# A second-attention-layer K tile group as seven block products, and a new order for all queues, on one Trainium2 core

## The chip, the core and the metric

The kernel runs on one core of one Trainium2 chip. The core has five instruction queues that run side by side: TensorE (PE, with its weight loads shown as PEld), VectorE (DVE), ScalarE (ACT), GpSimd (POOL) and SyncE (SP, which here only issues transfers). Each queue executes its instructions strictly in the order in which they were written; between queues there are only semaphores. The metric is the device time of the whole program in microseconds (us): the median of several runs. Beside it stands one profiled run, from which all durations come.

## The reference

The input is one sequence x of 2048 rows and 512 columns in bf16, with two sets of weights. Four layers follow each other: linear attention, feed-forward, and the same two once more with the same weights.

```python
x = x + attn(layernorm(x), wqkv, wo)     # layer 0
x = x + ffn(layernorm(x), w1, w2)        # layer 1
x = x + attn(layernorm(x), wqkv, wo)     # layer 2
x = x + ffn(layernorm(x), w1, w2)        # layer 3

def attn(x, wqkv, wo):                   # 32 heads of 16 columns
    q, k, v = split(x @ wqkv)
    phi = lambda t: where(t > 0, t + 1, exp(t)) + 1e-6
    kv  = sum over rows of phi(k)^T v    # 16 x 16 for each head
    z   = sum over rows of phi(k)
    return ((phi(q) @ kv) / (phi(q) @ z + 1e-6)) @ wo

def ffn(x, w1, w2):                      # 512 -> 1376 -> 512
    return maximum(x @ w1, 0) @ w2
```

## The kernel before, in words

The 2048 rows are held as 16 tiles of 128 rows, in four chunks of four tiles. Everything stays on the chip between the layers. In an attention layer each chunk is normalised, transposed (`Tb`), and multiplied with the K and Q columns of `wqkv`; `phi` of the K product is kept by tiles (`big`, used as PE's stationary operand later) and `phi` of the Q product by chunks. The products of `phi(k)` with the rows (`g0_*`, `g1_*`), the column sums (`zcol`, which becomes `Zc`), the head products (`kv*`, masked into `KVT` on DVE at L1133) and the merged matrix `Mf` (`m0` to `m3`, evicted at L1140 and L1141) form a barrier: the output of the layer (`fin*`, `ps<-Mf,big`) can only start when all rows have gone into them. For the denominator of chunk t, `den<t>` multiplies `phi(q)` by `Zc` (`ps<-big,Zc`), ACT takes a logarithm (`lnd<t>`, L1189) and an exponential of its negative (`rdc<t>`, L1191), SP spreads the result over the heads by four transfers of 128 KB (`spread<t>_*`, L1201, `big<-rdc`), and DVE multiplies two column blocks at a time (`pqs<t>_0` and `pqs<t>_2`, L1209). The `fin` products of chunk t need its two `pqs`.

The start is a special case. PE first multiplies a matrix of zeros by itself (`warm`, L793, `ps<-wrm`, WARM times 512 columns), and later eight times 128 columns (`fill0`, L816). The first tiles' statistics are DVE's `bnst<i>` and `bnag<i>` (L821, L822), ACT's `lnv<i>` and `rstd<i>` (L827, L829) and DVE's `fnorm<i>` (L859). The transposes of these tiles are made by PE (`trp<i>`, L888) and copied out of PSUM by ACT or DVE (L894, L895); those of later chunks by transfers (L874).

A block product replaces eight products of quarter matrices by seven, at the price of sums. In the feed-forward layers it is used for both matmuls, and in layer 2 for Q and K of chunks 0, 1 and 2. The list `A7` says which. A plain K chunk is four groups of four matmuls of 512 columns (`kproj12` to `kproj15`), each evicted by ACT once as t + 1 (L907) and once as exp(t) (L909) and joined on DVE (L915, L917). A block K chunk is seven groups (`k7_<chunk>_1` to `_7`) of four matmuls of 256 columns. Before them stand four sums of quarters of `Tb` on DVE (`as1` to `as4`, L996), which chunk by chunk serve Q and K alike; between them ACT copies one partial result into a second bank (`seed`, L681) and saves two (L1022), and DVE adds these back (L1042); ACT and DVE then do the same t + 1, exp, clamp and maximum (L1040, L1055, L1057, L1065, L1066).

The order is not that of the program's text. Every operation is entered into a graph with a name, and a list scheduler places the operations on each engine by priority:

```python
op.prio = op.idx + HINTS.get(op.key, 0)
...
pend = {e: sorted((o for o in ops if e in engs_of(o)), key=lambda o: (o.prio, o.idx)) for e in ENGINES}
```

`HINTS` has one number for each of some 1,850 operations (key: layer and name). An entry whose key ends in `!` picks the engine where an operation could go to several. The scheduler runs a model of the times to see what is ready and which PSUM bank comes free; its constants (`LOAD_LATE`, how late a load lands; the cost handed over with each matmul group) enter the order in that way and do nothing on the chip themselves. The result is one fixed order for each queue.

Of the kernel before, what the change touches and what calls it, by code (L numbers as in the profile page):

```python
# [52 lines left out]
LOAD_LATE = {"x1": -350.0, "x2": 190.0, "wka": 380.0, "wkb": 490.0, "wqa": 450.0, "x4": 500.0, "wqb": 510.0, "x12": 410.0, "x8": 260.0, "wv0": 350.0}  # L53
# [8 lines left out]
HINTS = {"0.as1": 50, "0.as3": 144, "0.as_h1": 145, "0.as_h2": 183, "0.as_id": 2, "0.bnag0": -4, "0.bnag1": -14, "0.bnag10":  # L62
# [525 lines left out]


def build_kernel(nc, A_x, A_wqkv, A_wo, B_w1, B_w2, out, n_layers_pairs=2, K_STT=0, Q_STT=0, windows=None,  # L590
                 WARM=10, SPLIT0=True, FIRST_PE_CHUNKS=2,
                 flex_strict=True, flex_bias_dve=0.0):
    FLEX_STRICT[0] = flex_strict
    FLEX_BIAS[DVE] = flex_bias_dve
# [16 lines left out]
    with es:  # L611
# [27 lines left out]
        Zc = sb("Zc", [128, 4, 32], BF16)  # L639
# [1292 lines left out]
```

## Time and profile before

| | us |
|---|---|
| median of 3 runs | 265.5 (265.16 to 266.06) |
| the profiled run's own time | 265.44 |
| its span, first to last instruction | 263.4 |
| outside the span | 2.04 |
| PE busy | 257.8 (98% of the span) |
| DVE busy | 225.7 (86%) |
| ACT busy | 198.8 (75%) |
| POOL busy | 59.4 (23%) |

The span is what the profile explains; the 2.04 us outside it are in every run. PE's busy time lies so near the span that the question at each place is whether PE waits there, and if it does, for which of the other queues. The chain of waits in the profile follows the last instruction back through what released it; where that chain is on PE for a long stretch, PE ran without a break. A row `178.09 12.22 PE L927 MATMUL ps<-Mf,big ... x55` of the timeline reads: starts at 178.09 us, lasts 12.22 us to the end of the last, matmuls of line 927 into PSUM from the stationary `Mf` and the moving `big`, 55 of them. Since matmuls overlap in the array, the spacing of n in a row is the length, less that of a single one, over n - 1.

### The profile page before, as it was taken

How to read it: one execution, taken by the hardware profiler on the slowest of the kernel's cores; microseconds unless marked ns; L12 is line 12 of the kernel's file. 1: busy time of each engine (PE TensorE's matmuls, PEld its weight loads, DVE VectorE, ACT ScalarE, POOL GpSimd, SP SyncE). 2: the span in 40 equal slices, each digit the busy share in tenths (PEclk: the TensorE clock that was granted, in tenths of full speed). 3: DMA queues.
4: the chain of work that ended last, by engine and by line, in shares of the span. 5: the costliest groups of instructions: out<-in, count | busy, mean ns of one | idle time of the engine just before them, and what ended most of it. 6: DMA issues, size and time to landing. Idle time of an engine off the chain costs nothing.

```text
span 263.4 us, 5741 instructions
## 1 busy us (share of the span) xinstructions
PE 257.8 (98%) x2130; PEld 194.2 (74%) x2130; DVE 225.7 (86%) x562; ACT 198.8 (75%) x429; POOL 59.4 (23%) x166
## 2 busy tenths in 40 slices
PE   7999999999999999999999999999999999999994
PEld 2744446844788898988888875574479988889883
DVE  4997795799999989998989988369998998888884
ACT  3999999469999888798998799776999943265000
POOL 1211000027942014122160430003891400000000
PEclk9999999999999999999999999999999999999999
DMA  6653982724415018232406031076437102400204
GB/s 218 260 147 76 256 317 64 178 54 93 91 43 102 1 20 122 40 24 43 39 0 82 0 64 20 2 163 157 80 60 141 24 2 81 80 2 35 67 0 162
DMA packets 45980, 22.46 MB, mean 85 GB/s; under 512 B 35872, under 2 KB 44416, under 8 KB 45952
## 3 DMA queue, kind: packets, MB, share of 16 engines
q1 hardware_dynamic: 45680, 21.83, 35.8%
q8 instruction: 17, 0.28, 0.4%
q10 hardware_dynamic: 272, 0.26, 0.4%
q14 instruction: 11, 0.09, 0.1%
HBM read 7.14 MB, written 2.10 MB: 35 GB/s over the span
## 4 chain that ended last, share of the span: by engine, by line
PE 93%; ACT 2%; DMA 2%; DVE 1%; issue 0%; SPq 0%; DVEq 0%
PE ps L927 92%; DMA big<-rdc 1%; DMA xin<-in_A_x_dram 1%; ACT rdc L1191 1%; PE ps L888 1%; ACT lnd L1189 1%; DVE bst L821 0%; DVE big L1209 0%; DVE big L1066 0%; ACT escr L909 0%; ACT GT L1121 0%; ACT big L907 0%; PE ps L816 0%; DVE rdc L1582 0%; DVE xn L859 0%
## 5 line engine op out<-in xcount | busy, mean ns | idle before, releaser
L942 ACT ACTIVATE sqscr<-xres 128x512 bf16<-128x512 f32 x48 | 29.9, 624 | 4.6 <-DVE xres L934 4.0
L681 ACT ACTIVATE ps<-ps 128x512 f32<-128x512 f32 (+1 forms) x38 | 20.6, 543 | 16.6 <-PE ps L927 13.4
L927 PE MATMUL ps<-w,big 128*128 128x256 bf16 (+1 forms) x256 | 32.7, 272 | 0.0
L927 PE MATMUL ps<-big,xn 128*128 128x256 bf16 (+1 forms) x224 | 32.1, 288 | 0.0
L927 PE MATMUL ps<-Mf,big 128*128 128x512 bf16 x128 | 28.5, 379 | 0.0
L927 PEld LDWEIGHTS ps<-w,big 128*128 128x128 bf16 (+1 forms) x256 | 25.0, 98 | 3.0
L927 PEld LDWEIGHTS ps<-big,xn 128*128 128x128 f16 x224 | 21.1, 98 | 7.5 <-issue 1.4
L927 PE MATMUL ps<-Tb,w 128*128 128x256 f16 x160 | 24.5, 273 | 0.0
L927 PE MATMUL ps<-Tb,wqkv 128*128 128x512 f16 (+1 forms) x120 | 23.5, 329 | 0.0
L927 PEld LDWEIGHTS ps<-Mf,big 128*128 128x128 bf16 x128 | 12.2, 98 | 15.3 <-ACT Mf L1140 0.9
L907 ACT ACTIVATE big<-ps 128x512 bf16<-128x512 f32 x40 | 23.0, 640 | 0.6 <-PE ps L927 0.6
L927 PE MATMUL ps<-xn,w 128*128 128x256 f16 x160 | 23.3, 272 | 0.0
L1398 ACT ACTIVATE big<-ps 128x512 bf16<-128x512 f32 (+1 forms) x32 | 17.0, 539 | 8.4 <-PE ps L927 8.2
L927 PE MATMUL ps<-xn,xin 128*128 128x256 f16 x160 | 23.2, 272 | 0.0
L927 PE MATMUL ps<-wqkv,Tb 128*128 128x512 bf16 (+1 forms) x104 | 23.0, 355 | 0.0
L851 POOL TENSOR_TENSOR rstd<-veps,nhalf 128x2 f32<-128x2 f32 x24 | 20.0, 835 | 11.4 <-DVE veps L849 10.4
L1410 DVE TENSOR_TENSOR big<-ps,escr 128x512 bf16<-128x512 f32 (+1 forms) x34 | 20.0, 590 | 2.6 <-PE ps L927 2.1
L1429 ACT ACTIVATE escr<-ps 128x512 f32<-128x512 f32 (+1 forms) x34 | 16.9, 522 | 2.4 <-PE ps L927 2.4
L927 PEld LDWEIGHTS ps<-Tb,wqkv 128*128 128x128 bf16 x120 | 11.6, 98 | 8.7 <-ACT Tb L894 0.4
L843 POOL TENSOR_SCALAR mean<-s 128x2 f32<-128x2 f32 x24 | 6.3, 263 | 49.9 <-DVE xres L934 48.7
L927 PEld LDWEIGHTS ps<-Tb,w 128*128 128x128 bf16 x160 | 15.2, 98 | 2.8 <-DVE w L1358 0.5
L927 PE MATMUL ps<-w,Tb 128*128 128x96 bf16 (+2 forms) x176 | 17.2, 224 | 0.0
(145 smaller groups left out, 599.2 us busy)
## 6 DMA issues: line engine op xcount, KB each, us to landing
big<-rdc SPq DMA_DIRECT2D x32, 128.0 KB, 2.7
xin<-in_A_x_dram SPq DMA_DIRECT2D x3, 512.0 KB, 6.8
w<-in_B_w_dram SPq DMA_DIRECT2D x1, 1376.0 KB, 7.1
w<-in_B_w_dram SPq DMA_DIRECT2D x1, 1280.0 KB, 10.2
wqkv<-in_A_wqkv_dram SPq DMA_DIRECT2D x3, 256.0 KB, 4.3
wqkv<-in_A_wqkv_dram SPq DMA_DIRECT2D x1, 512.0 KB, 4.2
wo<-in_A_wo_dram SPq DMA_DIRECT2D x1, 512.0 KB, 4.3
out_dram<-GT SPq DMA_DIRECT2D x1, 512.0 KB, 2.7
```

The costliest lines, as they stand in the source:

```text
L681: g.add(ACT, lambda e: e.activation(psv[:, b, 0:w], psv[:, src, 0:w], ACTF.Identity), [("ps", src)], [("ps", b)], C_ACT_PSUM if w == 512 e ...
L843: g.add(POOL, lambda e: e.tensor_scalar(mean[:, sl], s1[:, sl], -INV_D, None, ALU.mult), [("s1", i) for i in tl], [("mean", i) for i in tl ...
L851: g.add(POOL, lambda e: e.tensor_tensor(rstd[:, sl], veps[:, sl], nhalf[:, 0:n], ALU.pow), [("veps", lo), ("nhalf",)], [("rstd", i) for i ...
L888: last = e.transpose(psb()[:, 128 * c:128 * c + 128], xn[:, i, 128 * c:128 * c + 128], ident[:])
L907: ops = [g.add(ACT, lambda e: e.activation(dst_ap, psv[:, b, :], ACTF.Identity, bias=1.0 + 1e-6, scale=1.0), [("ps", b)], [dst_key], C_ACT ...
L927: last = e.matmul(o, l, r, start=st, stop=sp, skip_group_check=skip)
L942: g.add(ACT, lambda e: e.activation(sqscr[:, q, :], xres[:, i, :], ACTF.Square, scale=math.sqrt(INV_D), accum_out=s2[:, i:i + 1]), xr(i), ...
L1189: g.add(ACT, lambda e: e.activation(lnd[:, s, :], psv[:, b, :], ACTF.Ln, bias=1e-6, scale=1.0), [("ps", b)], [("lnd", s)], C_ACT_PSUM, nam ...
L1191: g.add(ACT, lambda e: e.activation(rdc[:, t, :], lnd[:, s, :], ACTF.Exp, scale=-1.0), [("lnd", s)], [("rdc", t)], C_ACT_SB, name="rdc%d" % t)
L1398: g.add_flex([(ACT, lambda e: e.activation(ap, src(), ACTF.Relu), C_ACT_PSUM if w == 512 else 270.0), (DVE, lambda e: e.tensor_scalar(ap, ...
L1410: g.add(DVE, lambda e: e.tensor_tensor(ap, sh(psv[:, bank, 0:w]), sh(other()), ALU.add), [("ps", bank)] + okeys + ([] if first else bk), q ...
L1429: g.add(ACT, lambda e, w=w: e.activation(q[:, 0:w], psv[:, bank, 0:w], ACTF.Identity), [("ps", bank)], key, C_ACT_PSUM if len(cs) == 2 els ...
```

## The change

The diff, without the some 1,630 numbers of `HINTS` that differ (76 of them choose another engine, nearly all between ACT and DVE; the two lines show the kind):

```diff
-LOAD_LATE = {"x1": -350.0, "x2": 190.0, "wka": 380.0, "wkb": 490.0, "wqa": 450.0, "x4": 500.0, "wqb": 510.0, "x12": 410.0, "x8": 260.0, "wv0": 350.0}
+LOAD_LATE = {"x1": 220.0, "x2": 500.0, "wka": 650.0, "wkb": 520.0, "wqa": 440.0, "x4": 1000.0, "wqb": 920.0, "x12": 760.0, "x8": 620.0, "wv0": 350.0}
...
-HINTS = {"0.as1": 50, "0.as3": 144, "0.as_h1": 145, "0.as_h2": 183, "0.as_id": 2, "0.bnag0": -4, "0.bnag1": -14, "0.bnag10":
+HINTS = {"0.as1": -7, "0.as3": -4, "0.as_h1": -14, "0.as_h2": -8, "0.as_id": 1, "0.bnag0": -2, "0.bnag1": -4, "0.bnag10": 38,
...
-                 WARM=10, SPLIT0=True, FIRST_PE_CHUNKS=2,
+                 WARM=8, SPLIT0=True, FIRST_PE_CHUNKS=2,
...
-        A7 = {0: [], 2: [('q', 0), ('q', 1), ('q', 2), ('k', 0), ('k', 1), ('k', 2)]}
+        A7 = {0: [], 2: [('q', 0), ('q', 1), ('q', 2), ('k', 0), ('k', 1), ('k', 2), ('k', 3)]}
...
             mm_group(lambda: [(psv[32 * j:32 * j + 32, b, :], Zc[:, j, :], unit_ap(pq_unit(j, t)), True, True, False) for j in range(4)],
-                     [("Zc",)] + [("big", pq_unit(j, t)) for j in range(4)], [("ps", b)], 330.0, "den%d" % t)
+                     [("Zc",)] + [("big", pq_unit(j, t)) for j in range(4)], [("ps", b)], 430.0, "den%d" % t)
```

So there are two changes to the work itself: K of chunk 3 in layer 2 becomes a block product (its sums `as1_3` to `as4_3` are new too, since Q of chunk 3 stays plain), and the zero matmuls at the start are eight instead of ten. All else is order.

**The start.** First DVE's queue from its first row, before and then after. `bst`, `mv`, `rstd` are the first tiles' statistics, `xin` the loaded input and `xn` the normalised tile.

```order
L786 MEMSET wrm 128x256
L821 BN_STATS bst<-xin 128x6 x2
L822 BN_AGGR mv<-bst 128x2 x2
L859 TENSOR_SCALAR xn<-xin,mv,rstd 128x512 x2
L821 BN_STATS bst<-xin 128x6
```

```order
L786 MEMSET wrm 128x256
L821 BN_STATS bst<-xin 128x6
L822 BN_AGGR mv<-bst 128x2
L821 BN_STATS bst<-xin 128x6
L822 BN_AGGR mv<-bst 128x2
L859 TENSOR_SCALAR xn<-xin,mv,rstd 128x512 x2
```

The first tile's `bnag0` now stands ahead of the second tile's `bnst1`, where both tiles' sums stood together. ACT's `lnv0` and `rstd0` correspondingly come ahead of `lnv1` and `rstd1`. Then PE's queue from its first row, before and after (`ident` is the identity of the transposes):

```order
L793 MATMUL ps<-wrm 128x512 x10
L888 MATMUL ps<-ident,xn 128x128 x8
L816 MATMUL ps<-wrm 128x128 x8
L927 MATMUL ps<-wqkv,Tb 128x512 x2
L927 MATMUL ps<-Tb,wqkv 128x256 x2
```

```order
L793 MATMUL ps<-wrm 128x512 x8
L888 MATMUL ps<-ident,xn 128x128 x4
L816 MATMUL ps<-wrm 128x128 x8
L888 MATMUL ps<-ident,xn 128x128 x4
L927 MATMUL ps<-wqkv,Tb 128x512 x8
```

The fill has moved between the two tiles' transposes, and the first projections are no longer K and Q by turns.

**K of chunk 3 in layer 2.** PE's queue near the end of the projections of layer 2. Before, the rows `ps<-wqkv,Tb 128x512` are `kproj12`, `kproj13` with `kproj15`, and `kproj14`; `ps<-big,xn` are `g0` and `g1`, `ps<-Tb,wqkv` is Q of chunk 3 (`qproj3_1`).

```order
L927 MATMUL ps<-wqkv,Tb 128x512 x4
L927 MATMUL ps<-big,xn 128x256 x4
L927 MATMUL ps<-wqkv,Tb 128x512 x8
L927 MATMUL ps<-big,xn 128x256 x4
L927 MATMUL ps<-wqkv,Tb 128x512 x4
L927 MATMUL ps<-Tb,wqkv 128x512 x4
```

After, from the second of the seven products on (the first stands three rows above): `ps<-wqkv,Tb 128x256` is `k7_3_2`, `ps<-GT,big ... x8` are `k7_3_5` and `k7_3_6`, `ps<-wqkv,big` is `k7_3_3`, the later `ps<-GT,big ... x4` is `k7_3_7` and `ps<-GT,Tb` is `k7_3_4`. `GT` holds sums of weights, `Mf` Q's; `ps<-Tb,Mf` belongs to Q of chunk 2, `ps<-Tb,wqkv` is Q of chunk 3.

```order
L927 MATMUL ps<-wqkv,Tb 128x256 x4
L927 MATMUL ps<-big,xn 128x512 x4
L927 MATMUL ps<-GT,big 128x256 x8
L927 MATMUL ps<-big,xn 128x256 x4
L927 MATMUL ps<-wqkv,big 128x256 x4
L927 MATMUL ps<-Tb,Mf 128x256 x4
L927 MATMUL ps<-GT,big 128x256 x4
L927 MATMUL ps<-big,xn 128x256 x4
L927 MATMUL ps<-Tb,wqkv 128x512 x4
L927 MATMUL ps<-GT,Tb 128x256 x4
```

Sixteen matmuls of 512 columns have become 28 of 256, and Q of chunk 3 now stands among the last of them.

**The barrier of layer 2.** DVE's queue around `den3`, before and after. The rows of L915 and L917 are clamp and maximum of Q of chunk 3 (the single `L917 ... big<-big,escr 128x512` behind an `L1209` is `q3_2_phi`); L1133 makes `KVT`, L1209 is a `pqs`, L1141 evicts `Mf`.

```order
L1133 TENSOR_TENSOR KVT<-ps,bmask 128x256
L917 TENSOR_TENSOR big<-big,escr 128x2x512
L1209 TENSOR_TENSOR big<-big 128x2x512
L915 TENSOR_SCALAR escr<-escr 128x512
L917 TENSOR_TENSOR big<-big,escr 128x512
L1209 TENSOR_TENSOR big<-big 128x2x512
L917 TENSOR_TENSOR big<-big,escr 128x512
L1133 TENSOR_TENSOR KVT<-ps,bmask 128x256
L1209 TENSOR_TENSOR big<-big 128x2x512
```

```order
L1133 TENSOR_TENSOR KVT<-ps,bmask 128x256
L915 TENSOR_SCALAR escr<-escr 128x512
L1209 TENSOR_TENSOR big<-big 128x2x512
L917 TENSOR_TENSOR big<-big,escr 128x512
L1141 CAST Mf<-ps 128x512
L1133 TENSOR_TENSOR KVT<-ps,bmask 128x256
L1209 TENSOR_TENSOR big<-big 128x2x512
L1141 CAST Mf<-ps 128x512
```

`q3_2_phi`, which `den3` needs, stood behind the second `pqs` (`pqs0_2`) and now stands ahead of it; `mev0` has come from ACT to DVE. Last, ACT's queue at the same place, before and after, each from `lnd1` on (`escr` and `big` are Q of chunk 3, `GT` an evicted sum, `Mf` the merged matrix):

```order
L1189 ACTIVATE lnd<-ps 128x512
L1191 ACTIVATE rdc<-lnd 128x512
L1189 ACTIVATE lnd<-ps 128x512
L907 ACTIVATE big<-ps 128x512
L1191 ACTIVATE rdc<-lnd 128x512
L907 ACTIVATE big<-ps 128x512
L909 ACTIVATE escr<-ps 128x512
L1121 ACTIVATE GT<-ps 128x2x256
```

```order
L1189 ACTIVATE lnd<-ps 128x512
L1191 ACTIVATE rdc<-lnd 128x512
L909 ACTIVATE escr<-ps 128x512
L1189 ACTIVATE lnd<-ps 128x512
L907 ACTIVATE big<-ps 128x512
L1121 ACTIVATE GT<-ps 128x2x256
L1121 ACTIVATE GT<-ps 128x256
L1140 ACTIVATE Mf<-ps 128x512
L1191 ACTIVATE rdc<-lnd 128x512
L1189 ACTIVATE lnd<-ps 128x512
```

`rdc2`, the second `L1191`, stood two rows behind `lnd2` and now stands five rows behind it, past the evictions of `GT` and one of `Mf`. On SP one transfer of chunk 3 (`spread3_2`) has moved ahead of two of chunk 2 (`spread2_2` and `spread2_3`).

584 rows, old and new, of the table HINTS are left out of this document.

## The prediction

> **What bounds the kernel now.** I read the page first: engine shares, then the chain of waits.
>
> ```profile
> span 263.4 us, 5741 instructions
> PE 257.8 (98%) x2130; PEld 194.2 (74%) x2130; DVE 225.7 (86%) x562; ACT 198.8 (75%) x429; POOL 59.4 (23%) x166
> PE 93%; ACT 2%; DMA 2%; DVE 1%; issue 0%; SPq 0%; DVEq 0%
> ```
>
> PE is the bound: 257.8 of 263.4 us. So only three things can move the time: what PE has to do, how late it begins, and the few places where it waits. The chain in order of time shows those places.
>
> ```profile
> 15.15 52.24 PE ps L927 x312
> ...
> 67.43 100.02 PE ps L927 x912
> ...
> 171.86 0.48 ACT lnd L1189
> 172.34 0.49 ACT big L907
> 172.83 0.53 ACT rdc L1191
> 173.36 0.14 SPq L1201
> ...
> 173.54 2.67 DMA big<-rdc
> ...
> 176.23 0.69 DVE big L1209
> 176.92 0.35 DVE big L917
> ...
> 177.31 10.44 PE ps L927 x50
> ...
> 187.77 72.00 PE ps L927 x676
> ```
>
> From 15.15 to 167 the chain is PE, with one hand-over at 67.43. It leaves PE before 177.31: there `den3` waited for `q3_2_phi` (0.35), which stood in DVE's queue behind `pqs0_2` (0.69), which waited for a spread (2.67). At 187.77 PE was again released by a `pqs`. From 187.77 to 259.8 it is PE without a break. Next the timeline of the start.
>
> ```profile
> 1.24 4.24 PE L793 MATMUL ps<-wrm 128*128 128x512 bf16 x10 [1.24 <-DVE wrm L786]
> 3.92 0.69 DVE L821 BATCH_NORM_STATS2 bst<-xin 128x6 f32<-128x512 bf16 x1 [0.35 <-DMA xin<-in_A_x_dram]
> 4.65 0.25 DVE L822 BATCH_NORM_AGGREGATE mv<-bst 128x2 f32<-128x6 f32 x2
> 4.87 0.30 ACT L827 ACTIVATE veps<-mv 128x1 f32<-128x1 f32 x2 [1.48 <-DVE mv L822]
> 5.11 0.30 ACT L829 ACTIVATE rstd<-veps 128x1 f32<-128x1 f32 x2
> 5.43 0.73 DVE L859 TENSOR_SCALAR xn<-xin,mv,rstd 128x512 f16<-128x512 bf16 x2 [0.53 <-ACT rstd L829]
> 5.91 0.72 PE L888 MATMUL ps<-ident,xn 128*128 128x128 f16 x8 [0.42 <-DVE xn L859]
> 6.34 1.08 ACT L894 ACTIVATE Tb<-ps 128x512 f16<-128x512 f16 x2 [0.94 <-PE ps L888]
> 6.46 0.61 PE L816 MATMUL ps<-wrm 128*128 128x128 bf16 x8
> 6.99 0.60 PE L927 MATMUL ps<-wqkv,Tb 128*128 128x512 bf16 x2
> ```
>
> Both tiles' `xn` waited for both tiles' statistics, so the first useful matmul stands at 6.99. A second reading matters later. Ten matmuls of 512 columns took 4.24 us, about 0.42 each. Set beside them the settled rate:
>
> ```profile
> 158.98 1.89 PE L927 MATMUL ps<-wqkv,Tb 128*128 128x512 bf16 x8
> 173.41 2.78 PE L927 MATMUL ps<-big,xn 128*128 128x256 bf16 x24
> ```
>
> Eight take 1.89 here. With about 0.38 for a single one the spacing is (1.89 - 0.38)/7 = 0.216 us; for 256 columns (2.78 - 0.27)/23 = 0.109. The zero matmuls thus ran at half the rate, while the fill at 6.46 (eight of 128 columns: (0.61 - 0.21)/7 = 0.057, about a quarter of 0.216) ran at the full one. The rate changed between the start of the tenth zero matmul, near 5.1, and about 5.9, which is 3.8 to 4.7 us after PE began.
>
> **The start.** Now `bnag0` stands ahead of `bnst1`. Worked with the durations above: the first tile's sums end before the second tile's input lands (3.92), `bnag0` ends near 3.8, `lnv0` and `rstd0` near 4.3 (each about 0.24 to the next). `fnorm0` must let `bnst1` and `bnag1` pass on DVE: 3.92 + 0.69 + 0.2 = 4.82. It ends at 5.25, and `trp0` starts at about 5.27 instead of 5.91. Its eviction, `kproj0_0` and what follows come 0.64 earlier, at 6.35; the fill between the two transposes takes 0.45 and covers the second tile, whose `xn` is ready near 5.75. Removing two zero matmuls alone gains nothing: the ten ended at 5.48, before `trp0` could start. But with `trp0` at 5.27 ten would be in its way, and eight (1.24 + 8 x 0.427 = 4.66) are not. The moved POOL steps (`ms_nhalf` later, `ms_hr` earlier) meet idle time there and I cost them at nothing.
>
> What is late next: ACT now does an exponential of K between `lnv2` and `rstd2` (0.62, a row is below), so the third tile's `xn` comes about 0.45 later, and PE, itself earlier, waits some 0.23 at `trp2`: the weights land when they did, and I put two such waits further on at 0.14 together, an estimate. The transposes by transfer (L874) have this row in a view of who waited for them:
>
> ```profile
>   PEld ps L927: 0.4, 2
> ```
>
> Two waits of PE cost 0.4; one is the hand-over at 15.15. More PE work stands ahead of it now, so I take half, 0.20, as absorbed. Sum: -0.64 + 0.23 + 0.14 - 0.20 = -0.47. The ends are 0 (PE held at 15.15 as now) and -0.84 (no new wait).
>
> **K of chunk 3.** PE: 16 x 0.216 = 3.45 leaves, 28 x 0.109 = 3.06 comes, -0.39 us; all of it on the path, PE being busy without a break there. What it adds elsewhere, by the groups of the page:
>
> ```profile
> L681 ACT ACTIVATE ps<-ps 128x512 f32<-128x512 f32 x30 | 17.6, 588 | 12.0 <-PE ps L927 9.0 <-DVE xres L1585 2.8
> L1022 ACT ACTIVATE lnd<-ps 128x512 f32<-128x512 f32 x6 | 3.4, 596 | 0.2 <-PE ps L927 0.2
> L1057 ACT ACTIVATE escr<-big,nbexp 128x512 bf16<-128x512 bf16 x12 | 8.4, 728 | 0.7 <-DVE big L1042 0.6
> L907 ACT ACTIVATE big<-ps 128x512 bf16<-128x512 f32 x40 | 23.0, 640 | 0.6 <-PE ps L927 0.6
> L909 ACT ACTIVATE escr<-ps 128x512 bf16<-128x512 f32 x24 | 13.7, 620 | 1.8 <-PE ps L927 0.8 <-DVE big L1066 0.8
> L996 DVE TENSOR_TENSOR big<-Tb 128x512 f16<-128x512 f16 x6 | 2.5, 419 | 0.3 <-DMA Tb<-xn 0.3
> L1042 DVE TENSOR_TENSOR big<-ps,lnd 128x512 bf16<-128x512 f32 x6 | 4.1, 682 | 0.2 <-PE ps L927 0.2
> L1065 DVE TENSOR_SCALAR escr<-escr 128x1024 bf16<-128x1024 bf16 x12 | 5.0, 422 | 0.8 <-ACT escr L1055 0.8
> L1066 DVE TENSOR_TENSOR big<-big,escr 128x1024 bf16<-128x1024 bf16 x12 | 8.0, 684 | 0.0
> L915 DVE TENSOR_SCALAR escr<-escr 128x512 bf16<-128x512 bf16 x10 | 2.7, 286 | 0.4 <-ACT escr L909 0.4
> L917 DVE TENSOR_TENSOR big<-big,escr 128x512 bf16<-128x512 bf16 x10 | 4.0, 419 | 0.0
> ```
>
> ACT had 4 x 0.64 + 4 x 0.62 = 5.0 us. It gets one seed, two saves, two linear parts, two exponentials from PSUM and two from SBUF: 0.59 + 1.19 + 1.28 + 1.24 + 1.46 = 5.8, so +0.7. DVE had 4 x (0.29 + 0.42) = 2.8; it gets four sums, two adds, two clamps, two maxima: 1.68 + 1.36 + 0.84 + 1.37 = 5.3, so +2.4. Is there room?
>
> ```profile
> 130.00:188.00 58.00, 57.74 (x445) 40.58 (x444) 47.94 (x123) 48.31 (x102) 15.98 (x47) 1.00 0.28 56
> ```
>
> In this stretch DVE works 47.9 of 58 us and ACT 48.3. With 50.4 and 49.0 both stay below PE's 57.4, and the four sums can be made long ahead. I cost them at nothing; if the cover is gone, `g0_3_3`, which needs the chunk's K, waits for one add, exponential, clamp and maximum (0.68 + 0.73 + 0.42 + 0.68 = 2.5 us at most).
>
> **The barrier.** `q3_2_phi` now stands ahead of `pqs0_2`, so `den3` no longer waits for a spread: PE idled 0.40 before it, all gained if nothing else is late, nothing if `mev0`, now on DVE, takes its place. I take the whole, since `q3_2`'s exponential also moved up on ACT. Against that, `rdc2` stands behind two exponential and linear parts of `q3_2`, three evictions of the barrier and so waits for PE's `m1`: about 176.7 instead of 173.36. Its spreads are issued thus:
>
> ```profile
> 170.78 11.15 SPq L1201 DMA_DIRECT2D big<-rdc  x15
> ```
>
> 15 take 11.15 us, so 0.74 each when they queue; each needs 2.67 more to land. `pqs2_2`, behind its last spread, then ends near the moment that `fin9_0` wants it, with some 0.15 to spare. I put the tight places together (`fin9`, `fin12` with its present 0.2, `fin0_2`, three block products of layer 3's chunk 2) at +0.25; between -0.2, where `fin12`'s present wait goes as well, and +0.74, one queued spread. The other reorderings of layers 1 and 3 change no work; I cost them at nothing, as PE's runs of 52, 100 and 72 us show that their queues were ahead.
>
> **The sum.** 265.44 (profiled) - 0.47 - 0.39 - 0.40 + 0.25 = 264.43. The profiled run stands 0.06 under the median of 265.5, so I say 264.4.
>
> **Rivals.**
>
> First, the clock. Eight zero matmuls end at 4.66 and PE then idles 0.6 us, before the rate had changed in the profiled run (5.1 or later). Speaking for it: the rise took 3.8 to 4.7 us of nearly unbroken work. If the pause starts that count anew at 5.27, the full rate comes at 9.1 to 10.0, and for that time every matmul takes double: half of 3.8 to 4.7 is 1.9 to 2.35, less the 0.37 of waits at `trp2` and for weights that it fills: 1.5 to 2.0, so with the 264.4 of the forecast 265.9 to 266.4, taken as 266.2. It decides from a full rate at about 8.2 on: half of 2.9 us, less 0.37, has eaten the 1.1 us. Slower by 0.8 needs a full rate no earlier than about 9.8. Speaking against: a pause of 0.42 stood in the old stretch too (before 5.91), and the rate was full behind it.
>
> [...]
>
> Second, the start's gain is eaten by loads. Everything from 15.15 on hangs together with transposes by transfer. For it: the hand-over at 15.15 waited for one, and no transfer is issued sooner unless its tiles are normalised sooner. If PE is held there as now, the 0.47 are gone: 264.9.
>
> Third, the spreads. If `pqs2_2` and `pqs3_0` are one queued spread later than I worked out, `fin9` and what follows wait 0.74 more: 265.2. For it: `spread3_2`, which needs the late `rdc3`, now stands ahead of two spreads of chunk 2 in SP's queue. Against it: eight `fin` steps of 0.86 stand between.
>
> **How the numbers follow.** Forecast 264.4, 0.47 (its own range 263.7 to 264.7); loads 264.9, 0.18; spreads 265.2, 0.15; clock 266.2, 0.20. A difference under 0.3% (0.8 us) can't be told from no change here. Faster (under 264.7): 0.47 and 0.03 of the loads' case, 0.50. Same (264.7 to 266.3): 0.15 + 0.12 + 0.08 = 0.35. Slower: 0.12 of the clock's case and 0.03 of the spreads', 0.15. The low end takes all terms at their best: 265.44 - 0.84 - 0.39 - 0.40 - 0.2 = 263.6; the high end is the clock's 266.2.
>
> **What would show it.** Right: `trp0` at 5.3 and its matmuls spaced 0.056, the first K matmul near 6.35; 28 rows of 256 columns in place of the 16; no wait before `den3`; the chain unbroken to the `fin` steps. Wrong: first transposes spaced 0.107; a PE wait on `pqs2_2` or `pqs3_0`, longer than 0.3; a wait of `g0_3_3` for L1066; or new waits in layers 1 and 3, which I cost at nothing.

## The result, and the profile after

The changed kernel takes 264.06 us (median of 6 runs, 263.72 to 264.37) against 265.38 (265.16 to 266.06, 6 runs) of the kernel before: a ratio of 0.9946, with an interval of 0.9931 to 0.9962. That is 1.32 us, or 0.54%. The forecast was 264.4, a gain of 1.1. The number was right, but by luck: most of the terms behind it came out worse, new waits in layer 1 that had been put at nothing cost 0.8, and gains that were not in the sum at all paid for that, as the traces show.

First the page of the kernel after, its own time being 264.34:

```profile
span 262.6 us, 5778 instructions
PE 255.9 (97%) x2131; PEld 194.7 (74%) x2140; DVE 227.7 (87%) x568; ACT 202.1 (77%) x438; POOL 58.5 (22%) x154
PE 74%; DVE 14%; DMA 4%; issue 2%; SPq 2%; ACT 1%; DVEq 0%
```

PE is still the bound, with 1.9 us less busy time (of which two zero matmuls are 0.8, K of chunk 3 and the three `den` below 0.4 each, by their rows), but the chain that ends last is PE for 74% only, where it was 93%. DVE has 14% of it. The chain in order of time shows where:

```profile
60.67 0.69 DVE big L1209
...
69.65 0.58 DVE veps L849
...
77.45 76.57 PE ps L927 x718
154.08 12.99 PE ps L927 x95
167.12 6.15 PE ps L927 x55
186.12 0.49 DVE nbias L853
...
187.22 1.22 DVE big L1209 x2
188.49 71.13 PE ps L927 x672
```

At the outputs of layer 0 and the start of layer 1 (60 to 71 us), and at the outputs of layer 2 (to 188.5), it is DVE that PE follows now. Between 77 and 173, K of chunk 3 included, PE runs without a break. PE's waits besides the first one, which is that for the zeros, again after:

```profile
PE ps L888 <- DVE xn L859: 0.5, 1, 0.5
PE ps L927 <- DVE big L1209: 0.5, 1, 0.5
PE ps L927 <- DVE w L1358: 0.5, 1, 0.5
PE ps L927 <- DMA wqkv<-in_A_wqkv_dram: 0.4, 1, 0.4
```

The wait for `xn` is the first transpose's and existed before (0.4). The one for L1209 is before the last chunk's outputs of layer 2. The one for `w` is the first matmul of layer 1 that needs a sum made on DVE, and the last is the second half of the Q weights.

The span, read in four stretches from both traces, divides as follows:

| stretch, to | before | after | change in it | made of |
|---|---|---|---|---|
| first matmul of layer 1 | 67.43 | 67.60 | +0.17 | start -0.25, wait for `w` 0.62 where 0.20 stood before |
| `den3` of layer 2 | 177.31 | 176.69 | -0.79 | K of chunk 3 -0.39, wait at `den3` -0.32, `den0` to `den2` -0.41, DVE's waits in layer 1 +0.35 |
| last matmul's end | 259.76 | 259.62 | +0.48 | wait at the last outputs 0.63 where 0.18 stood before |
| span's end | 263.4 | 262.6 | -0.6 | the last stores |

A wait is counted here by the starts: by how much later a matmul starts than the spacing (0.216 us behind 512 columns, 0.109 behind 256, 0.056 behind 128) lets it start. The idle time in the brackets of the rows is some 0.17 shorter. The terms add up to each stretch within 0.05; the span's end is read to 0.1. A further 0.3 lies outside the span (2.04 before, 1.74 after; between 1.7 and 2.1 over all runs of this study) and stays unexplained.

The rows at `den3`, before and then after:

```profile
176.68 0.39 PE L927 MATMUL ps<-GT,wqkv 128*128 128x128 bf16 x4
177.31 0.40 PE L927 MATMUL ps<-big,Zc 128*32 128x512 bf16 x4 [0.24 <-DVE big L917]
```

```profile
176.15 0.61 PE L927 MATMUL ps<-GT,wqkv 128*128 128x128 bf16 x8
176.69 0.40 PE L927 MATMUL ps<-big,Zc 128*32 128x512 bf16 x4
```

Before, `den3` starts 0.63 after the first of four matmuls of 128 columns, 0.41 more than their 0.22. After, it starts 0.54 after the first of eight, 0.09 more than their 0.45; those 0.09 stand ahead of every `den`, waiting or not. So 0.32 of the wait went.

**The start.** The timeline of the first 10 us, after:

```profile
1.24 3.44 PE L793 MATMUL ps<-wrm 128*128 128x512 bf16 x8 [1.24 <-DVE wrm L786]
5.22 0.40 PE L888 MATMUL ps<-ident,xn 128*128 128x128 f16 x4 [0.55 <-DVE xn L859]
5.46 0.61 PE L816 MATMUL ps<-wrm 128*128 128x128 bf16 x8
...
6.31 1.90 PE L927 MATMUL ps<-wqkv,Tb 128*128 128x512 bf16 x8
...
10.07 0.61 PE L927 MATMUL ps<-Tb,wqkv 128*128 128x256 f16 x4 [0.43 <-DMA wqkv<-in_A_wqkv_dram]
```

`trp0` starts at 5.22 and the first K matmul at 6.31 (worked out: 5.27 and 6.35). Here the full rate held from `trp0` on (the fill of eight is again 0.61 long), so the clock's rival did not happen in this run. At 10.07 the transfer of the Q weights takes 0.43 of idle time back, 0.60 by the starts.

**The three `den`.** Where they stood one by one between `g` products, they stand now in one row. First before, then after, from the timeline:

```profile
168.26 0.40 PE L927 MATMUL ps<-big,Zc 128*32 128x512 bf16 x4
```

```profile
169.70 0.83 PE L927 MATMUL ps<-big,Zc 128*32 128x512 bf16 x12
170.47 1.92 PE L927 MATMUL ps<-big,xn 128*128 128x256 bf16 x16
```

Three groups of four, which use 32 columns of the array each, take 0.77 from the first start to that of the next work, not three times some 0.4.

**DVE's small steps.** DVE and POOL at the start of layer 1 and at the outputs of layer 2, after:

```profile
69.16 1.05 POOL L864 TENSOR_SCALAR xn<-xres,mean,rstd 128x512 f16<-128x512 f32 x1
69.57 0.66 DVE L849 TENSOR_SCALAR veps<-var 128x2 f32<-128x2 f32 x1
...
72.15 0.16 DVE L849 TENSOR_SCALAR veps<-var 128x2 f32<-128x2 f32 x1
...
185.84 0.77 POOL L864 TENSOR_SCALAR xn<-xres,mean,rstd 128x512 f16<-128x512 f32 x1
186.04 0.57 DVE L853 TENSOR_TENSOR nbias<-mean,rstd 128x2 f32<-128x2 f32 x1
```

A step on 128x2 numbers takes 0.16 on DVE at 72.15. The two other steps of that size here take 0.66 and 0.57, and each ends with POOL's normalisation of a tile (70.23 and 70.21; 186.61 and 186.61). Two more like them stand at 63.10 and 74.16, 0.53 and 0.52 long, and these end with a normalisation on POOL too (within 0.02). Together the four are 1.65 us of DVE's time above what they need. The new order had put two of them (`var4` and `veps8`, the steps at 63.10 and 69.57) on DVE, where POOL did them before. The other two (`veps12` and `nbias2`) were DVE's before as well, but met no normalisation there: each took 0.16 (at 79.22 and 186.33; POOL's next tile came at 186.40). Such steps (`var`, `veps`, `nbias`) are 30 of the 76 entries of `HINTS` that choose another engine, so the remark under the diff that nearly all of these are between ACT and DVE is not right. Not every step of DVE is drawn out so: before, a residual of 128x512 (L934, at 186.41) took its usual 0.68 beside the tile at 186.40. Why the four were, the traces do not show; they show the ends that coincide.

**The end.** The last stores, in the view of the transfers between 259 and 263 us (kind: packets, MB, share); before, then after:

```profile
q1 hardware_dynamic: 731, 0.57, 44.6%
q8 instruction: 1, 0.02, 1.5%
```

```profile
q1 hardware_dynamic: 723, 0.54, 40.9%
```

Instructions are themselves fetched by transfers: the page has 17 on the queue q8 (`instruction: 17, 0.28` MB, so 16 KB each) in both runs. That they are PE's is read from their places: between two of them PE starts 226 to 293 instructions, nearly all matmuls and weight loads, in both traces, though the time between them goes from 12 to 23 us. Before, the last piece came at 259.78 to 260.71, among the last stores; after, it came at 256.82. From the last matmul to the end it took 3.6 us before and 3.0 after, and the stores of 64 KB landed after 2.1 us before and 1.6 after. Why the piece comes earlier is not shown: the kernel after has ten matmuls more in PE's stream, but the kernel below that takes K of chunk 3 out again has two fewer than before, and there it comes early too. In no row of the kernel's own instructions does that cause appear.

### The profile page after: what moved, and what is told of

It reads as the page before. It is cut to its first block, busy times and chain, and to the rows that moved or that the text cites. A ratio compares the mean times of both kernels' runs of the same rounds, so it can differ in the third digit from the quotient of the medians.

```text
span 262.6 us, 5778 instructions
## 1 busy us (share of the span) xinstructions
PE 255.9 (97%) x2131; PEld 194.7 (74%) x2140; DVE 227.7 (87%) x568; ACT 202.1 (77%) x438; POOL 58.5 (22%) x154
## 4 chain that ended last, share of the span: by engine, by line
PE 74%; DVE 14%; DMA 4%; issue 2%; SPq 2%; ACT 1%; DVEq 0%
PE ps L927 74%; DVE xres L934 4%; DMA wqkv<-in_A_wqkv_dram 2%; DMA big<-rdc 2%; DVE big L1209 2%; DVE bst L821 2%; DVE xn L859 1%; SPq L1201 1%; DVE xn L1376 1%; DVE escr L915 1%; DVE big L1410 1%; SPq L737 1%; DVE wqkv L1084 1%; ACT escr L909 0%; DVE veps L849 0%
## 5 line engine op out<-in xcount | busy, mean ns | idle before, releaser
L927 PE MATMUL ps<-big,xn 128*128 128x256 bf16 (+1 forms) x222 | 30.8, 287 | 0.1
L927 PE MATMUL ps<-xn,xin 128*128 128x256 f16 x160 | 22.4, 273 | 0.1
L907 ACT ACTIVATE big<-ps 128x512 bf16<-128x512 f32 x36 | 21.6, 676 | 0.0
L1398 ACT ACTIVATE big<-ps 128x512 bf16<-128x512 f32 (+1 forms) x39 | 20.3, 535 | 1.5 <-PE ps L927 1.2
L851 POOL TENSOR_TENSOR rstd<-veps,nhalf 128x2 f32<-128x2 f32 x24 | 18.5, 770 | 12.5 <-DVE veps L849 11.5
L843 POOL TENSOR_SCALAR mean<-s 128x2 f32<-128x2 f32 x24 | 8.5, 356 | 54.3 <-DVE xres L934 52.6
L927 PE MATMUL ps<-wqkv,Tb 128*128 128x512 bf16 (+1 forms) x93 | 20.0, 343 | 0.2
```

Of the source, the lines that this page charges most:

```text
L843: g.add(POOL, lambda e: e.tensor_scalar(mean[:, sl], s1[:, sl], -INV_D, None, ALU.mult), [("s1", i) for i in tl], [("mean", i) for i in tl ...
L851: g.add(POOL, lambda e: e.tensor_tensor(rstd[:, sl], veps[:, sl], nhalf[:, 0:n], ALU.pow), [("veps", lo), ("nhalf",)], [("rstd", i) for i ...
L907: ops = [g.add(ACT, lambda e: e.activation(dst_ap, psv[:, b, :], ACTF.Identity, bias=1.0 + 1e-6, scale=1.0), [("ps", b)], [dst_key], C_ACT ...
L927: last = e.matmul(o, l, r, start=st, stop=sp, skip_group_check=skip)
L1398: g.add_flex([(ACT, lambda e: e.activation(ap, src(), ACTF.Relu), C_ACT_PSUM if w == 512 else 270.0), (DVE, lambda e: e.tensor_scalar(ap, ...
```

## The experiments

Each ratio is to the kernel before, run on the same chip, with its 95% interval behind it. A small function `_moved` in some of them takes the first operation of a pair out of its engine's finished order and puts it right ahead of the second; nothing else of the order changes.

**The last stores.** On the kernel before, some products near the end of layer 3 are cut in two, so that PE has more instructions in front of its end and the last fetch comes earlier.

```diff
+                    if halves and not st:
+                        e.matmul(o[:, 0:128], l, r[:, 0:128], start=st, stop=sp, skip_group_check=skip)
+                        o, r = o[:, 128:256], r[:, 128:256]
...
+            halves = g.layer == 3 and name in ("p6_2_0", "p7_2_0")
```

> The kernel before with two late groups of the last layer (p6_2_0 and p7_2_0, at 246 to 249 us) in matmuls of 128 columns instead of 256, but for the first of each: the same products, some 20 matmuls and weight loads more in PE's stream, PE's time about 0.05 more by the spacings of 0.057 and 0.109. If the last fetch of instructions is what holds up the last stores: it comes 2 us or more earlier, the part from the last matmul to the end falls from 3.6 to 3.0, and the time by 0.5, to 264.9. If not: 3.6 and 265.4 to 265.5.

264.78 us; ratio 0.998 (0.9965 to 0.9994). The fetch came at 253.97, the time from the last matmul to the end fell from 3.6 to 3.0, and the last matmul itself ended at 259.46 (259.76 before). So 0.6 us of the stores hang on where one 16 KB piece lands, with no change to the stores. A second way of moving the fetches is to cut the zero matmuls of the start into quarters:

```diff
-                for k in range(WARM):
-                    last = e.matmul(psv[:, wt, :], wrm[:, 0:128], wrm[:, :], start=True, stop=True)
+                for k in range(4 * WARM):
+                    last = e.matmul(psv[:, wt, 0:128], wrm[:, 0:128], wrm[:, 0:128], start=True, stop=True)
```

> The kernel before, its ten zero matmuls of 512 columns cut into forty of 128: as much zero work, 30 matmuls and 30 weight loads more in PE's stream, no other edit. In the profile of before a 16 KB fetch of instructions lies at 259.8 to 260.7 us, on the last stores, and the time from the last matmul to the end is 3.6 us; where the fetch lies elsewhere it is 3.0. If the fetch is the cause: it comes some 3 us earlier against the end, the last part falls from 3.6 to 3.0, and the time by 0.5 to 0.6, to about 264.9. If the last part has another cause (where the stores lie, the order of the transfers): it stays at 3.6 and the time at 265.5.

267.95 us; ratio 1.01 (1.0064 to 1.0137). The end did get shorter (3.0, last fetch at 256.95), but the time that was expected, 264.9, was missed by 3 us: the last matmul ended 3.4 later. This time all 17 pieces moved, and three of them fell on small transfers that PE was waiting for. One of these, from the transfers between 50.5 and 51.8 us and the timeline after it:

```profile
q8 instruction: 1, 0.02, 4.6%
...
big<-rdc SPq DMA_DIRECT2D x2, 128.0 KB, 3.4
```

```profile
52.94 0.69 DVE L1209 TENSOR_TENSOR big<-big 128x1024 bf16<-128x1024 bf16 x1 [0.68 <-DMA big<-rdc]
```

The spread took 3.4 us where 2.7 is usual, and the outputs of layer 0 waited 0.57 more than before. Two transposes by transfer, at 71.6 and 85.4, landed 1.3 and 1.65 later, and PE waited 0.46 and 0.87 there. These three make 1.9 of the 3.4. The rest (0.4 at the start, a wait of 0.6 at 24.62, 0.9 in two at 208 to 209, 0.3 at 233, less 0.7 of waits of before that are gone) is not traced to a fetch. Over the kernels of this study the end's length goes by the fetch:

| kernel | last fetch's start, against the last matmul's end | from there to the span's end |
|---|---|---|
| before | +0.02 | 3.6 |
| before, `q3_2_phi` moved (below) | +0.03 | 3.6 |
| before, products cut | -5.50 | 3.0 |
| before, zero matmuls cut | -6.23 | 3.0 |
| after | -2.80 | 3.0 |
| after, with four other edits (`den`, `pqs`, small steps, below) | -2.74 to -2.82 | 3.0 |
| K of chunk 3 put in or taken out (below) | -2.81, -2.51 | 3.0 |
| Q weights first, four zero matmuls, layer 2's order (below) | -2.79, -2.33, -2.86 | 3.0 |

So a piece cost time where it met a transfer that something waited for: 0.6 at the last stores, and 0.57, 0.46 and 0.87 of PE's time at the three small ones above. Seven pieces fell between 77 and 173 us of the kernel after, where PE ran without a break; none of them cost PE anything there.

**DVE's small steps.** The four go to POOL in the kernel after:

```diff
+HINTS.update({'0.var4!': 0, '0.veps8!': 0, '0.veps12!': 0, '2.nbias2!': 0})
```

> The changed kernel with four small statistics steps (var4, veps8 and veps12 behind layer 0, nbias2 behind layer 2; 128 x 2 numbers each) on GpSimd instead of VectorE, nothing else moved. In its profile each of them took 0.45 to 0.58 us on VectorE and ended in the same moment as a normalisation (norm3, norm7, norm11, norm3) on GpSimd. If VectorE's queue, held up there, is what PE waits for at usum3 (0.3 to 0.6), hs2_1 (0.3) and pqs3_0 (0.6): these waits shrink by 0.37, 0.3 and 0.41, and the time falls by about 1 to 263.1. If the steps only come later on GpSimd and the normalised tiles with them: the waits move to the transposes, and the time stays at 264.1.

262.96 us (262.53 to 263.26); ratio 0.9908 (0.9889 to 0.9926). That is 1.1 us under the changed kernel's median and beats both. The waits of PE are down to one small one beside the first:

```profile
PE ps L890 <- DVE xn L861: 0.2, 1, 0.2
```

The wait for `w` in layer 1 is gone, and so is that of `hs2_1`. The first matmul of layer 1 and the outputs of layer 2 now read (compare 67.60 after; the break that stood at 188.49 after would lie inside the second row, four matmuls ahead of its end):

```profile
66.83 1.04 PE L929 MATMUL ps<-Tb,w 128*128 128x256 f16 x8
...
177.79 10.01 PE L929 MATMUL ps<-Mf,big 128*128 128x512 bf16 x44
```

So the new waits of the kernel after, in layer 1 and at layer 2's outputs, came from four steps of 0.16 us that took 0.5 or more beside POOL's normalisations.

**The three `den`.** `den1` and `den2` are put one `g` group apart again, in the kernel after:

```diff
+MOVES = [("2.g0_2_3", "2.den1"), ("2.g0_1_3", "2.den2")]
```

> The changed kernel with den0, den1 and den2 apart again on PE: g0_2_3 between the first two, g0_1_3 between the last two, nothing else. The traces of before and after give 0.42 for each of three denominators between other products (0.33 to the next start and 0.09 of a gap ahead) and 0.86 for three in a row, so 0.4 of PE's time. If VectorE sets the pace of the output steps behind (the wait for pqs3_0, 0.64): that wait takes the 0.4 up and the time stays within 0.2 of 264.1. If PE sets it: 264.5.

264.39 us; ratio 0.9957 (0.9939 to 0.9975). The timeline of it:

```profile
169.41 0.40 PE L949 MATMUL ps<-big,Zc 128*32 128x512 bf16 x4
169.75 0.61 PE L949 MATMUL ps<-big,xn 128*128 128x256 bf16 x4
170.28 0.40 PE L949 MATMUL ps<-big,Zc 128*32 128x512 bf16 x4
```

Between 168 and 178.5 PE needed 0.44 more for the same matmuls. The wait at the last outputs was 0.58 all the same (0.63 after): what PE loses ahead of it is not taken out of that wait, presumably since the reciprocals and their spreads start from the same `den`. In the median only 0.3 of it is seen, against runs that vary by more. So the same edit was made on the kernel without the waits.

```diff
+HINTS.update({'0.var4!': 0, '0.veps8!': 0, '0.veps12!': 0, '2.nbias2!': 0})
+MOVES = [("2.g0_2_3", "2.den1"), ("2.g0_1_3", "2.den2")]
```

> The same with the four small steps on GpSimd, so that VectorE isn't late: 263.0 and what the three denominators apart cost when nothing hides it, 0.3 to 0.4, so 263.35. If three in a row are no cheaper than three apart: 263.0.

263.56 us; ratio 0.992 (0.9898 to 0.9943), 0.6 above the one with them together by the medians, 0.3 by the ratios; in the stretch itself PE needed 0.44 more. Twelve matmuls of 32 columns in one row are worth about 0.4 here.

**The last outputs of layer 2.** The two `pqs` of chunk 3 go ahead of two residuals and of `nbias2` on DVE, in the kernel after:

```diff
+MOVES = [("2.pqs3_2", "2.resid7"), ("2.pqs3_0", "2.resid7")]
```

> The changed kernel with pqs3_2 and pqs3_0 moved ahead of resid7, nbias2 and resid9 on DVE. If DVE's order alone makes PE wait 0.6 us before fin15: pqs3_0 ends 1.2 us earlier, the wait goes, and the time falls by 0.5 to 0.6, to 263.5. If the residuals that are now later hold up PE in their turn (banks, or the first tiles of layer 3): a wait of 0.3 or more appears within the next 5 us of PE and the time stays at 264.0.

264.44 us; ratio 0.9952 (0.9932 to 0.9971), no gain over the kernel after. The wait at the outputs went, and layer 3 waited instead, first here, then in five smaller places:

```profile
192.31 0.61 PE L949 MATMUL ps<-Tb,w 128*128 128x256 f16 x4 [0.25 <-ACT ps L703]
```

The last matmul ended at 259.67, as against 259.62. DVE had no room: the busy times between 178 and 190 us (PE, PEld, DVE, ACT, POOL, the clock, the transfers' share and GB/s), before and after, are

```profile
178.00:190.00 12.00, 11.98 (x57) 5.19 (x55) 11.23 (x32) 9.32 (x23) 7.00 (x19) 1.00 0.53 118
```

```profile
178.00:190.00 12.00, 11.48 (x55) 5.10 (x54) 12.00 (x33) 9.85 (x26) 7.61 (x20) 1.00 0.62 135
```

DVE was busy for all of the 12 us after. In this full queue the other order chose who waited. That the two residuals, which now came later, are what held layer 3 up is argued and not shown: the row names a copy on ACT. `nbias2` took 0.15 in this run, so its 0.4 less alone gained nothing here, while the run above gained with the residuals in their places.

**K of chunk 3, alone.** First into the kernel before, with the places of the new operations as the kernel after has them, and nothing else:

```diff
-        A7 = {0: [], 2: [('q', 0), ('q', 1), ('q', 2), ('k', 0), ('k', 1), ('k', 2)]}
+        A7 = {0: [], 2: [('q', 0), ('q', 1), ('q', 2), ('k', 0), ('k', 1), ('k', 2), ('k', 3)]}
+HINTS.update({'2.as1_3': -6, '2.as1_3!': 0, '2.as2_3': -3, '2.as2_3!': 0, '2.as3_3': 7,
...
```

> The kernel before with K of chunk 3 in layer 2 as a block product and nothing else moved outside that stretch. If PE is the bound there and the sums are covered: 28 matmuls of 256 columns in place of 16 of 512, 0.39 us off, 265.4 to 265.0, and no new wait of PE between 150 and 167 us. If DVE or ACT lack the room (the rival): PE waits at g0_3_3 or at the den steps and the time stays at 265.3 or above. The profile also shows whether the last stores of the kernel before always take the 3.6 us from the last matmul to the end that its profile showed.

269.52 us; ratio 1.0142 (1.0103 to 1.018). Nearly 4 us lost, with 0.39 less of PE's work:

```profile
158.83 0.61 PE L929 MATMUL ps<-wqkv,Tb 128*128 128x256 bf16 x4 [0.23 <-ACT ps L683]
159.92 0.61 PE L929 MATMUL ps<-GT,big 128*128 128x256 bf16 x4 [0.48 <-DVE big L998]
...
168.32 1.04 PE L929 MATMUL ps<-big,xn 128*128 128x512 bf16 x4 [1.49 <-DVE big L1068]
```

The seven products stood in a row here, and their sums (L998) and a saved part (L683) each came too late; at 168.32 `g0_3_3` waits for the last maximum of K (1.65 by the starts). In the kernel after, products of `g0` and `g1` stand between the seven. The next run takes only the block product out of the kernel after and gives the plain chunk's operations their numbers from the kernel before:

```diff
-        A7 = {0: [], 2: [('q', 0), ('q', 1), ('q', 2), ('k', 0), ('k', 1), ('k', 2), ('k', 3)]}
+        A7 = {0: [], 2: [('q', 0), ('q', 1), ('q', 2), ('k', 0), ('k', 1), ('k', 2)]}
+HINTS.update({'2.k12_em': 12, '2.k12_exp': -9, '2.k12_lin': -11, '2.k12_phi': 15,
...
```

> The changed kernel with K of chunk 3 plain again. If that part is worth its PE time: 264.06 + 0.39 = 264.45. If it was swallowed by a later wait on DVE (the wait of 0.6 us before the last output steps of layer 2): 264.06, with that wait shorter by about 0.4.

265.57 us; ratio 0.9988 (0.9967 to 1.001). Part of what comes back is PE's 0.39, part a new wait of 0.48 by the starts before a block of Q (the profile names ACT for 0.32 of it):

```profile
164.57 1.04 PE L929 MATMUL ps<-Tb,wqkv 128*128 128x512 f16 x4 [0.32 <-ACT big L909]
```

The last matmul ended 0.73 later (260.35) than with the block product. So inside the new order the block product is worth its 0.39 and the absence of that wait, 0.73 in the trace, and 1.1 us by the two ratios (0.9988 and 0.9946), whose intervals together leave room for some 0.7 less or more. That is more than the 0.39 that had been expected of it. Then the 415 numbers of layer 2 by which the kernel after differs, with the block product, were put into the kernel before:

```diff
+HINTS.update({'2.aksum1': -364, '2.aksum2': -356, '2.aksum3': -363, '2.aksum4': -169,
...
-        A7 = {0: [], 2: [('q', 0), ('q', 1), ('q', 2), ('k', 0), ('k', 1), ('k', 2)]}
+        A7 = {0: [], 2: [('q', 0), ('q', 1), ('q', 2), ('k', 0), ('k', 1), ('k', 2), ('k', 3)]}
...
-                     [("Zc",)] + [("big", pq_unit(j, t)) for j in range(4)], [("ps", b)], 330.0, "den%d" % t)
+                     [("Zc",)] + [("big", pq_unit(j, t)) for j in range(4)], [("ps", b)], 430.0, "den%d" % t)
```

> The kernel before with the whole of layer 2 in the changed kernel's order, K of chunk 3 as a block product with it; layers 0, 1 and 3 in their own. If the changed order of layer 2 is what makes room for the block product: no PE wait between 156 and 170 us, den3 and m3 without waits (0.34 less), K 0.39 less, fin15 waiting 0.45 more than fin12 did, so PE ends 0.3 earlier, and the time is 264.5 to 265.2, according to where the last fetch of instructions falls. If the room came from layer 1: waits for the sums or for phi as in the block product alone, 266 or more.

274.61 us; ratio 1.0339 (1.0316 to 1.0362). The waits stand before the place that was meant, from layer 1 on, the two longest of them here:

```profile
148.95 0.72 PE L929 MATMUL ps<-xin,xn 128*128 128x256 bf16 x5 [1.58 <-DVE Tb L1485]
...
159.72 0.61 PE L929 MATMUL ps<-GT,big 128*128 128x256 bf16 x4 [1.15 <-ACT lnd L1024]
```

Layer 1's chunks are still being finished when layer 2's sums are made, on the same queues; here one layer's order did not fit the other's. As a test of K of chunk 3 this run says little, except that at 165 to 177 its sums were not late.

**The barrier.** `q3_2_phi` ahead of `pqs0_2` on DVE, in the kernel before and alone:

```diff
+MOVES = [("2.q3_2_phi", "2.pqs0_2")]
```

> The kernel before with q3_2_phi moved ahead of pqs0_2 on DVE, nothing else. If PE's wait before den3 is time on the path: it goes, and the time falls by 0.25 to 0.4, to 265.0 to 265.15. If the outputs behind it are set by DVE's queue (the rival): pqs3_2 comes when it came, the wait of 0.18 at fin12 grows by what den3 gained, and the time stays at 265.4.

265.78 us; ratio 1.0 (0.9974 to 1.0025).

```profile
177.31 0.40 PE L949 MATMUL ps<-big,Zc 128*32 128x512 bf16 x4
177.42 0.42 DVE L1155 TENSOR_TENSOR KVT<-ps,bmask 128x256 bf16<-128x256 f32 x1 [0.18 <-PE ps L949]
177.90 0.60 PE L949 MATMUL ps<-wo,KVT 128*128 128x512 bf16 x2 [0.19 <-DVE KVT L1155]
```

`den3` does not wait any more, but `pqs0_2` (0.69) now stands ahead of a mask (L1155), and `m3` waits for that, 0.25 by the starts where 0.32 was saved. Alone, the step is worth nothing; it takes the place of the mask as well, which the kernel after gives in its order.

**The start.** In the kernel after, the second half of the Q weights is loaded ahead of the input's second chunk:

```diff
-        ld_x(4, 8)
         ld_w(slice(0, D), "wqb", slice(2, 4))
+        ld_x(4, 8)
```

> The changed kernel with the second half of Q's weights loaded ahead of tiles 4 to 7, nothing else. If the start's gain is lost to that load (PE waits 0.3 to 0.6 us for it near 10 us): the wait goes, and PE stands 0.3 to 0.5 earlier at 10.6 us. If the later tiles then hold PE up in turn: a wait of about the same length at trp4 or at the transposes near 15 us, and nothing is left at 30 us. In the time it is 0.3 at most either way: 263.8 to 264.4.

264.23 us; ratio 0.9952 (0.9937 to 0.9968), the same as after. The weights landed at 8.19 instead of 10.02 and the wait went. But this run's fill took 1.06 instead of 0.61, the first K matmul came at 6.75, and a later tile's transpose came 0.2 late: layer 0's last product ended at 67.49, not sooner than the 67.14 after. And with half the zero matmuls:

```diff
-                 WARM=8, SPLIT0=True, FIRST_PE_CHUNKS=2,
+                 WARM=4, SPLIT0=True, FIRST_PE_CHUNKS=2,
```

> The changed kernel with four zero matmuls instead of eight, so that PE stands still from 2.9 to 5.2 us. If the pause starts the count of the clock anew (the clock rival of the prediction): transposes, fill and projections at half rate until about 9 to 10 us, with a loss of 1.5 us or more less the wait for Q's weights that it fills (0.6), 264.9 to 265.5. If the rate rises some 4 us after PE's first instruction whatever it does in between: full rate at the first transposes and 264.1.

265.49 us; ratio 0.9996 (0.9977 to 1.0014): the whole gain of the change lost.

```profile
1.24 1.89 PE L793 MATMUL ps<-wrm 128*128 128x512 bf16 x4 [1.24 <-DVE wrm L786]
5.04 0.61 PE L888 MATMUL ps<-ident,xn 128*128 128x128 f16 x4 [1.92 <-DVE xn L859]
...
6.72 3.62 PE L927 MATMUL ps<-wqkv,Tb 128*128 128x512 bf16 x8
10.14 0.67 PE L927 MATMUL ps<-Tb,wqkv 128*128 128x256 f16 x4
```

Eight matmuls of 512 columns take 3.62 where 1.90 stood, so all of them ran at half the rate, 0.43 apart and not 0.216; the full one comes near 10.1. The last matmul ends 1.06 later (260.68).

## Why the prediction was right, point by point

- **What bounds the kernel: right.** PE's work and waits, with the end of the span, account for the result to 0.05 in each stretch of the span. But the wording that "only three things can move the time" left out a fourth, what follows PE's last instruction: 0.6 of the 0.8 that the span fell.
- **The start, -0.47: a little less came.** Worked out to 0.05 as far as the first K matmul, but so close by chance: it came at 6.24 to 6.75 in seven traces with the new start and at 6.62 to 7.05 in five with the old one (medians 6.47 and 6.99, -0.52 where -0.64 had been worked out). No run takes DVE's new order out by itself. Of the new waits, that at `trp2` was smaller (0.10, not 0.23), and the weights cost 0.60 where two waits together had been put at 0.14. The end of layer 0's last product moved by 0.25 between the two profiles (67.39 and 67.14); over five kernels with the old start and six with the new its medians are 67.55 and 67.18, -0.37. The 0.20 at 15.15 came nearly whole, though its row is one of weight loads (PEld) and not of PE's waits: before, the matmul there started 0.17 late by the spacing, and after no matmul between 11 and 18 us does.
- **K of chunk 3, -0.39 on PE, nothing elsewhere: right in the kernel after**, where no wait for its sums or its maximum is seen. The run with the old order shows what the cover was, as far as the two traces go: the places of the seven products between others, without which `g0_3_3` waits 1.65 and four products 2.0 together. No run changed these places alone. That wait of `g0_3_3` was named, with a bound of 2.5. The room in DVE and ACT over 58 us, from which it was costed at nothing, said nothing on whether a sum is in time.
- **The barrier, -0.40: 0.32 came at `den3`.** The 0.40 counted the 0.09 that stays ahead of every `den`. The condition "if nothing else is late" was the weak point: alone the step gives nothing, because the mask is late next. The prediction had thought of `mev0`, not of the mask of `m3`.
- **The tight places of the outputs, +0.25: too small.** 0.45 came, of the ends -0.2 to +0.74. The cause given (spreads in SP's queue) was not it: DVE was full, and one of its small steps took 0.57 where it met POOL's normalisation. Nor does a queued spread cost the 0.74 of the upper end: where they follow without a break they are issued about 0.65 apart (172.24, 172.89, 173.54 before); the row's mean had pauses in it.
- **"The other reorderings of layers 1 and 3 change no work; I cost them at nothing": the step that failed.** They move small steps between POOL and DVE or to where they meet POOL's normalisation, and 0.8 of new waits in layer 1 followed (0.42 and 0.35). That an unbroken stretch of PE shows its queues to be ahead was true of the old order only.
- **Not in the sum: the three `den` in one row, -0.4, and the last stores, -0.6.** The first could be read from the instruction order and the length of a group of four before; the second from nothing in the page but the fetch among the last transfers.
- **The rivals.** What the forecast calls the clock is read here from the spacing of the matmuls. The half rate did not come back in the profile of the kernel after, but it does with four zero matmuls (265.49, where the rival's case had been put at 266.2). No run had shown whether a pause delays the rise, so the rival's 0.20 was an estimate of the author's. With 1.89 us of zero matmuls and a pause of 1.92 the full rate came near 10.1. With 3.44 to 3.6 us of them and a pause of 0.15 to 0.77 it stood from the first transposes on in four traces (5.15 to 5.61), and came near 6 in two others and near 7 in one, in all seven before the 8.2 from which on the forecast saw the gain eaten. The run with four changed the work and the pause together and does not tell which of them it was. The loads took part of the start's gain. The spreads did not decide.

So the total agreed to 0.3 us by luck: 1.3 of losses had been missed (0.8 in layer 1, 0.2 at the outputs, 0.2 at the start, 0.1 at the barrier) and 1.3 of gains (0.4 of the `den`, 0.6 of the stores, 0.3 outside the span). A right total does not show that the terms are right.

## What to carry to other kernels

An order given by a table also decides which engine does the smallest steps; look where these stand against another engine's long operations. Here four of 0.16 us took 0.52 to 0.66 beside POOL's normalisations, and moving them was worth nearly as much as the whole change. Look also at what is not in the kernel's own rows: cutting some 20 matmuls in two moved the last fetch of instructions from 259.78 to 253.97 us, and one that met the last stores or a small transfer cost 0.5 to 0.9 us here. And try a part of a schedule only with the places of what surrounds it: of this change, the block product alone cost 4 us and layer 2's order alone 9.

## What was not expected of the hardware

- A DVE step on 128x2 numbers, 0.16 us by itself, took 0.52 to 0.66 in the four places where POOL normalised a tile of 128x512 beside it (0.77 to 1.05), and ended with it.
- Where a 16 KB fetch of instructions (0.9 to 1.4 us long in the traces of before and after) met the last stores, the end took 0.6 longer; a spread that met one landed 0.7 later, and two transposes by transfer 1.3 and 1.65.
- Matmuls on 32 columns of the array: 12 in a row took 0.83 us, while each four of them between full-width matmuls took about 0.12 to 0.15 more than a third of that.
